# One kernel of attention and routed experts: new instruction ranks, an earlier strike, contiguous list columns and a halved eviction

## The chip, the cores and the metric

The kernel runs on one core of one Trainium2 chip. Its time is the device time of one launch in microseconds (us). Three runs of the kernel before gave 716.53, 718.13 and 720.70 us; the median is 718.13. The engines are called as in the profile: PE (TensorE's matmuls), PEld (its weight loads), DVE (VectorE), ACT (ScalarE), POOL (GpSimd) and SP (SyncE, which only issues DMAs).

## The reference

Inputs: q, k, v of 8 batches x 8 heads x 576 positions x 64, a gate of 512 x 8, and two weight tensors of 8 experts (512 x 1024 and 1024 x 512), all fp32.

```python
# attention: a coarse one on means of 4 positions, and a local one
q_d, k_d, v_d = (t.reshape(B, H, Sd, 4, D).mean(axis=3) for t in (q, k, v))
out_up = np.repeat(sm_attn(q_d, k_d, v_d), 4, axis=2)
mask = np.abs(pos[:, None] - pos[None, :]) < 4          # 7 neighbours
out_local = softmax(where(mask, scale * q @ k.T, -1e9)) @ v
x = (out_up + out_local) -> (4608 tokens, 512)
# experts: all (token, expert) logits in falling order; a token goes to the
# first expert that has room (576 places each)
for idx in np.argsort(-(x @ w_gate).flatten()):
    tok, e = idx // E, idx % E
    if assigned[tok] >= 0 or counts[e] >= cap: continue
    assigned[tok] = e; counts[e] += 1
out[mask_e] = np.maximum(x[mask_e] @ w1[e], 0) @ w2[e]
```

So every token gets one expert, every expert exactly 576 tokens, and who gets which depends on all logits at once.

## The kernel before

**Two stages.** Class `Attention` works through 8 batches and 36 units of 128 tokens. Per batch it loads q, k, v, transposes q and k, forms sums of four and does the coarse attention, whose result goes to a DRAM tensor `up_dram`. Per unit it loads the windows of v (stream W), computes local scores (S), transposes (T), products with v and the normalisation (V), loads the repeated coarse rows (P, `load_up`), adds them (A, on DVE, for units 27 to 33 on POOL), stores x (D) and computes logits (X). Stream Z0 prepares the routing of units 0 to 25 while the attention still runs, Z1 that of the last ten.

The second stage takes the experts in the order in which they fill up. For k = 0 to 7: `Routing.pre` (stream S: row maxima m of the logits, sortable integers s, their high and low halves spread by ACT into xh and xl, one-hot masks, first compares), `phase` (R: a search for the threshold at which the first expert is full, in three levels of 64, 32 and 32 on the high half and three on the low half; each level compares, counts on PE, clips the counts (cs, line 832), sums them on PE, finds the first full one (un) and feeds the next threshold), then `emit` or, for k = 0, `emit_first`: ranks of the chosen tokens, two one-hot tables (ohh from the rank's high part, ohl from its low part), and 18 or 36 matmuls of them (the list) that put the token numbers in order. `gather` (G) fetches the tokens' rows on POOL, five chunks of 128, 128, 128, 128 and 64; `rows` (X) scales them to fp16 high and low parts; `weights` (L) loads and `split` (W) splits the expert's weights the same way (ACT the high, DVE the low part, 8 tiles); `first` (H), `relu` (E), `second` (C) and `store` (Y) are the expert itself: three products (high-high, high-low, low-high) for each layer, ReLU with a new split on ACT and DVE, eviction by ACT, and a scatter by POOL.

**The strike.** When expert k is full, its column is taken out of the logits: DVE makes the mask es (line 1048), POOL multiplies it by -1e30 (line 1060) and adds it to all logits (line 1061). This stands in `end`, which comes after the ranks; `left` (line 1044) is called before them. The next expert's row maxima (line 912) read the logits.

**The order of the work.** Each stream is a generator whose steps are cut by `yield`. `KEYS` holds one rank for each step of each stream; `Plan.run` always takes the step of lowest rank and, through `need`, first whatever this step depends on. In the first stage this order holds for all engines, in the second for PE, DVE, ACT and SP, while POOL's order is left to the framework's planner. Each engine executes its own instructions in the order in which they were issued. A step beyond the end of its stream's ranks gets the last rank plus 0.01 for each further step (`key`). Z0 has 16 steps, Z1 11.

**The first list.** In `emit_first` the low one-hot table is laid out with the low position outside and the token column t inside, so the weights of matmul t are `ohl[:, :, t]`, every 36th element; the compare is made in two halves of 18 columns (`EH`). The tile is lent from the expert's `ht`. FILL gives numbers of matmuls without use that keep TensorE busy while the routing waits.

**The eviction.** `Experts.store` scales each chunk out of PSUM on ACT (line 1419). The last chunk of an expert has 64 rows, computed in two halves of PSUM's partitions, so DVE adds the second half (line 1422). Then POOL scatters the rows.

Of the kernel before, what the change touches and what calls it, by code (L numbers as in the profile page):

```python
# [710 lines left out]
class Routing:  # L711
# [68 lines left out]
    def lend(self, raw):  # L780
# [3 lines left out]
        self.ohw, self.lent = raw[:, :128].bitcast(BF), (raw[:, 82:100].bitcast(BF), raw[:, 100:136].bitcast(BF))  # L784
# [190 lines left out]
    def phase(self, plan, k):  # L975
# [68 lines left out]
        def left():  # L1044
            nc.vector.tensor_tensor(rem, cl, low[0], op=OP.subtract)

        def end(rank):
            nc.vector.tensor_scalar(es, self.code, code, None, op0=OP.is_equal)
# [10 lines left out]
            if k < E - 2:  # L1059
                nc.gpsimd.tensor_scalar(self.pen, es, -1e30, None, op0=OP.mult)  # L1060
                nc.gpsimd.tensor_tensor(self.lg, self.lg, self.pen[:, None].to_broadcast([128, NT, E]), op=OP.add)
# [74 lines left out]
    def emit_first(self, plan, ph, pl):  # L1136
# [9 lines left out]
        ohl = self.ohw  # L1146
        p = self.ps.tile([128, 72], F32, name="pR", bufs=2)[:, :36]
        for i, (a, b) in enumerate(EH):
            if i:
                yield  # L1150
            nc.vector.tensor_tensor(ohl[:, :32, a:b], pl[:, None, a:b].to_broadcast([128, 32, b - a]), self.slot[:, :, a:b],
                                    op=OP.is_equal)
            yield
            self.fill("half" if i else "list")
            for t in range(a, b):
                nc.tensor.matmul(p, ohl[:, :, t], r[:, :, :, t], start=t == 0, stop=t == NT - 1)
# [43 lines left out]
class Experts:  # L1200
# [210 lines left out]
    def store(self, k):  # L1411
# [3 lines left out]
        for c, (s0, n) in enumerate(SL):  # L1415
# [3 lines left out]
            nc.scalar.activation(y[:n], p[:n], AF.Copy, scale=sc)  # L1419
            if n < 128:  # L1420
                yield
                nc.vector.scalar_tensor_tensor(y[:n], p[64:], sc, y[:n], op0=OP.mult, op1=OP.add)
# [756 lines left out]
```

## Time and profile before

| | |
|---|---|
| median of three runs | 718.13 us |
| profiled execution | 716.23 us |
| its span, first to last instruction | 714.6 us |
| PE busy | 674.7 us (94%) |
| PEld busy | 487.5 us |
| DVE busy | 485.8 us (68%) |
| ACT busy | 349.0 us |
| POOL busy | 248.4 us |
| HBM read, written | 93.08 MB, 21.23 MB |
| attention, routing of the first expert, experts (starts) | 0, 257.5, 281.3 us |

The busy time of an engine is the sum of its instructions' durations; matmuls overlap, so a PE that is busy is not one at its peak. In a row of the timeline the brackets at the end give the idle time of the engine before the instruction and what ended it. "PEclk" is the clock that TensorE was granted, as a share of 2.4 GHz. A line number (L1347) is that of the kernel before.

### The profile page before, as it was taken

How to read it: one execution, taken by the hardware profiler on the slowest of the kernel's cores; microseconds unless marked ns; L12 is line 12 of the kernel's file. 1: busy time of each engine (PE TensorE's matmuls, PEld its weight loads, DVE VectorE, ACT ScalarE, POOL GpSimd, SP SyncE). 2: the span in 40 equal slices, each digit the busy share in tenths (PEclk: the TensorE clock that was granted, in tenths of full speed). 3: DMA queues.
4: the chain of work that ended last, by engine and by line, in shares of the span. 5: the costliest groups of instructions: out<-in, count | busy, mean ns of one | idle time of the engine just before them, and what ended most of it. 6: DMA issues, size and time to landing. Idle time of an engine off the chain costs nothing.

```text
span 714.6 us, 19791 instructions
## 1 busy us (share of the span) xinstructions
PE 674.7 (94%) x8031; PEld 487.5 (68%) x8031; DVE 485.8 (68%) x1284; ACT 349.0 (49%) x692; POOL 248.4 (35%) x295
## 2 busy tenths in 40 slices
PE   6999999999999988799999989999999999999994
PEld 4888888898888866574575566576575674764741
DVE  5677777666767666899998798797796776510300
ACT  6587688687686532434435153353442463411310
POOL 7477284537564521204223140330511504102011
PEclk9699999999999976999999999999999999999998
DMA  7799899898898733517774452760931994301001
GB/s 209 203 246 248 231 285 256 262 264 216 258 236 244 224 122 134 169 39 264 135 264 117 176 189 61 274 150 14 337 98 50 407 215 128 72 1 53 15 30 37
DMA packets 142723, 123.86 MB, mean 173 GB/s; under 512 B 86752, under 2 KB 116960, under 8 KB 142632
## 3 DMA queue, kind: packets, MB, share of 16 engines
q1 hardware_dynamic: 135256, 100.82, 49.7%
q0 software_dynamic: 6512, 21.24, 9.4%
q8 instruction: 63, 1.03, 0.6%
q10 hardware_dynamic: 864, 0.54, 0.3%
q14 instruction: 28, 0.23, 0.1%
HBM read 93.08 MB, written 21.23 MB: 160 GB/s over the span
## 4 chain that ended last, share of the span: by engine, by line
PE 51%; issue 18%; DVE 11%; DMA 9%; ACT 4%; POOL 3%; SPq 1%; POOLq 0%; ACTq 0%; DVEq 0%
PE pX L1402 15%; PE pH L1347 14%; DMA up<-up_dram 6%; PE g L502 3%; PE o L554 2%; PE g L353 2%; DMA nat<-in_k_dram 2%; POOL out_dram L1423 2%; PE g L593 2%; PE g L531 2%; PE g L292 2%; PE pR L828 2%; ACT kt L271 1%; PE g L607 1%; DVE x L576 1%
## 5 line engine op out<-in xcount | busy, mean ns | idle before, releaser
L1347 PE MATMUL pH<-xt,wh 128*128 128x256 f16 (+1 forms) x1024 | 192.6, 288 | 2.8 <-DVE ht L1379 2.8
L1402 PE MATMUL pX<-wh,ht 128*128 128x512 f16 (+1 forms) x640 | 183.0, 379 | 0.0
L1347 PE MATMUL pH<-xt,wl 128*128 128x320 f16 (+1 forms) x512 | 145.2, 288 | 0.0
L1402 PEld LDWEIGHTS <-ht 128*128 128x128 f16 (+1 forms) x960 | 81.6, 100 | 87.3 <-issue 3.0
L1402 PE MATMUL pX<-wl,ht 128*128 128x512 f16 (+1 forms) x320 | 117.9, 380 | 0.0
L1423 POOL DMA_INDIRECT out_dram<-y,idx x40 | 43.3, 1081 | 210.6 <-ACT y L1419 193.7
L1347 PEld LDWEIGHTS <-wh 128*128 128x128 f16 x1024 | 95.3, 98 | 29.9 <-DVE ht L1379 3.8
L1375 ACT ACTIVATE ht<-pH 128x512 f16<-128x512 f32 (+1 forms) x128 | 45.5, 407 | 119.5 <-PE pH L1347 106.3
L1379 DVE SCALAR_TENSOR_TENSOR ht<-pH,ht 128x512 f16<-128x512 f32 (+1 forms) x128 | 52.3, 450 | 60.8 <-ACT ht L1375 60.6
L1256 DVE SCALAR_TENSOR_TENSOR wl<-nat,wh 128x512 f16<-128x512 f32 x128 | 86.4, 684 | 4.5 <-ACT wh L1251 3.9
L1279 POOL DMA_INDIRECT xg<-x_dram,idx x40 | 47.4, 1186 | 81.6 <-issue 34.5
L1251 ACT ACTIVATE wh<-nat 128x1024 f16<-128x1024 f32 x64 | 67.0, 1056 | 6.8 <-DMA nat<-in_moe_w_dram 6.0
L1419 ACT ACTIVATE y<-pX 128x512 f32<-128x512 f32 (+1 forms) x40 | 23.8, 596 | 92.2 <-PE pX L1402 55.9
L1347 PEld LDWEIGHTS <-wl 128*128 128x128 f16 x512 | 50.4, 98 | 13.2
L258 POOL TENSOR_TENSOR gtmp<-qz 64x576 f32<-64x576 f32 x28 | 32.8, 1172 | 64.3 <-ACT qz L340 39.3
L539 ACT COPY pt<-g 64x512 f32<-64x512 f32 x72 | 41.6, 580 | 15.3 <-PE g L531 13.6
L502 PE MATMUL g<-kt,qz 128*64 128x38 f32 x1152 | 44.0, 232 | 1.2 <-ACT kt L271 0.8
L502 PEld LDWEIGHTS g<-kt,qz 128*64 128x64 f32 x1152 | 43.0, 145 | 3.2 <-issue 1.7
L554 PE MATMUL o<-vw,pt 128*64 128x65 f32 x1152 | 43.4, 224 | 0.2 <-DMA nat<-in_k_dram 0.2
L292 PE MATMUL g<-ident,nat 128*128 128x128 f32 x256 | 36.7, 281 | 4.9 <-DMA nat<-in_k_dram 3.9
L554 PEld LDWEIGHTS o<-vw,pt 128*64 128x64 f32 x1152 | 37.9, 137 | 5.1 <-issue 4.2
L271 ACT COPY kt<-g 64x512 f32<-64x512 f32 x50 | 31.4, 630 | 7.4 <-PE g L292 6.5
(225 smaller groups left out, 1121.3 us busy)
## 6 DMA issues: line engine op xcount, KB each, us to landing
nat<-in_moe_w_dram SPq DMA_DIRECT2D x28, 1024.0 KB
vw<-in_v_dram SPq DMA_DIRECT2D x136, 78.0 KB
up<-up_dram SPq DMA_DIRECT2D x36, 256.0 KB
x_dram<-x SPq DMA_DIRECT2D x36, 256.0 KB
nat<-in_q_dram SPq DMA_DIRECT2D x16, 512.0 KB
nat<-in_k_dram SPq DMA_DIRECT2D x16, 512.0 KB
nat<-in_v_dram SPq DMA_DIRECT2D x16, 512.0 KB
up_dram<-xu SPq DMA_DIRECT2D x16, 128.0 KB
```

Of the source, the lines that this page charges most:

```text
L292: nc.tensor.transpose(p[:, a, :, fp], src[:, 4 * hh + 2 * a + s, 2 * fp:2 * fp + 2].rearrange("p f d -> p (f d)"), self.ident)
L502: nc.tensor.matmul(sv[64 * a:64 * a + 64, 4 * g + c], self.qz[b % 2][:, 2 * g + a, w].rearrange("p s q -> p (s q)"), self.kt[b][:, 2 * g + ...
L539: nc.scalar.copy(out[r, :, :, a], p[r].rearrange("p (i h q) -> p i h q", h=4, q=QW))
L554: nc.tensor.matmul(o[64 * i:64 * i + 64, g, 65 * h:65 * h + 65], pt[:, 2 * g + i, h].rearrange("p b q -> p (b q)"), self.vw[u % 4][:, i, 4 ...
L1251: nc.scalar.activation(hi, r, AF.Copy, scale=sc)
L1256: nc.vector.scalar_tensor_tensor(lo[:, a:a + LOP], r[:, a:a + LOP], sc, hi[:, a:a + LOP], op0=OP.mult, op1=OP.subtract)
L1279: self.fetched = self.nc.gpsimd.indirect_dma_start(out=xg[:n], out_offset=None, in_=self.x, in_offset=bass.IndirectOffsetOnAxis(ap=idx[:n, ...
L1347: nc.tensor.matmul(p[:, s, :s1 - s0], self.w[k, d][a][:, 128 * f:128 * f + 128], self.xt[k][:, b, d, s0:s1], start=j == 0, stop=j == len(s ...
L1375: nc.scalar.activation(hi, q, AF.Relu)
L1379: nc.vector.scalar_tensor_tensor(lo, q, 0.0, hi, op0=OP.max, op1=OP.subtract)
L1402: nc.tensor.matmul(p[o:o + m], self.ht[k][:, f, h0:h0 + m], self.w[k, 4 + f // 2][b][:, 512 * (f % 2):512 * (f % 2) + 512], start=j < part ...
L1423: i = nc.gpsimd.indirect_dma_start(out=self.out, in_=y[:n], in_offset=None, out_offset=bass.IndirectOffsetOnAxis(ap=plan.vals["idx", k][:n ...
```

## The change

Four edits of code and a new table. (1) The instruction that makes es and the two POOL instructions of the strike go from `end` to the beginning of `left`. (2) In `emit_first` the low one-hot table is laid out with the token column outside, so that the 128 weights of matmul t are contiguous; 32 of them are its own, the other 96 belong to the next columns, and what they produce in PSUM isn't read. The first half's matmuls stop three columns early, since a matmul reads three columns further. (3) The last chunk of the last expert is evicted in two halves of 256 columns. (4) All ranks in `KEYS` are replaced, those of the attention by a table in which Z0 has 11 entries and Z1 nine.

```diff
-        self.ohw, self.lent = raw[:, :128].bitcast(BF), (...)
+        self.ohw, self.lent = raw[:, :36].rearrange("p i t -> p (i t)").bitcast(BF), (...)
...
         def left():
+            nc.vector.tensor_scalar(es, self.code, code, None, op0=OP.is_equal)
+            if k < E - 2:
+                nc.gpsimd.tensor_scalar(self.pen, es, -1e30, None, op0=OP.mult)
+                nc.gpsimd.tensor_tensor(self.lg, self.lg, self.pen[:, None].to_broadcast([128, NT, E]), op=OP.add)
             nc.vector.tensor_tensor(rem, cl, low[0], op=OP.subtract)
         def end(rank):
-            nc.vector.tensor_scalar(es, self.code, code, None, op0=OP.is_equal)
...
-            if k < E - 2:
-                nc.gpsimd.tensor_scalar(self.pen, es, -1e30, None, op0=OP.mult)
-                nc.gpsimd.tensor_tensor(self.lg, self.lg, self.pen[:, None].to_broadcast([128, NT, E]), op=OP.add)
...
-        ohl = self.ohw
+        ohl = self.ohw[:, :32 * NT].rearrange("p (t i) -> p t i", i=32)
...
-            nc.vector.tensor_tensor(ohl[:, :32, a:b], pl[:, None, a:b].to_broadcast([128, 32, b - a]), self.slot[:, :, a:b],
-                                    op=OP.is_equal)
+            nc.vector.tensor_tensor(ohl[:, a:b], pl[:, a:b, None].to_broadcast([128, b - a, 32]),
+                                    self.io[:, None, :].to_broadcast([128, b - a, 32]), op=OP.is_equal)
...
-            for t in range(a, b):
-                nc.tensor.matmul(p, ohl[:, :, t], r[:, :, :, t], start=t == 0, stop=t == NT - 1)
+            for t in range(max(0, a - 3), b if i else b - 3):
+                nc.tensor.matmul(p, self.ohw[:, 32 * t:32 * t + 128], r[:, :, :, t], start=t == 0, stop=t == NT - 1)
...
-            nc.scalar.activation(y[:n], p[:n], AF.Copy, scale=sc)
+            cols = [slice(0, 512)] if n == 128 or k < E - 1 else [slice(0, 256), slice(256, 512)]
+            for w in cols:
+                nc.scalar.activation(y[:n, w], p[:n, w], AF.Copy, scale=sc)
             if n < 128:
                 yield
-                nc.vector.scalar_tensor_tensor(y[:n], p[64:], sc, y[:n], op0=OP.mult, op1=OP.add)
+                for w in cols:
+                    nc.vector.scalar_tensor_tensor(y[:n, w], p[64:, w], sc, y[:n, w], op0=OP.mult, op1=OP.add)
```

Of the table (598 streams), the entries at the start, cut where "..." stands:

```diff
-    "Z0": [1797, 1807, 1828, 1838, 1843, 1853, 1863, 1869, 1879, 1889, 1900, 1906, 1916, 1922, 1925, 1942],
+    "Z0": [1822, 1835, 1842, 1849, 1860, 1866, 1878, 1882, 1895, 1905, 1908],
-    "S0": [2, 9],
+    "S0": [2, 3],
-    "R0": [0, 1, 3, 4, 5, 6, 7, 8, 10, 11, 12, ...
+    "R0": [0, 1, 4, 5, 6, 7, 8, 9, 10, 11, 12, ...
-    "S1": [59, 61, 64, 66, 69, 73, 75, 78, 79, 81, 84, 91],
+    "S1": [57, 60, 61, 63, 66, 67, 69, 70, 73, 75, 80, 86],
-    "R1": [94, 95, 101, 103, 104, 107, 108, 110, 112, ...
+    "R1": [84, 85, 92, 95, 96, 99, 104, 108, 110, ...
-    "X0": [70, 72, 76, 77, 80, 82, 83, 85, 89, 90, 93, 97, 100, 102, 105, 106],
+    "X0": [74, 76, 78, 79, 81, 82, 83, 87, 90, 91, 93, 97, 98, 101, 106, 107],
-    "H0": [86, 87, 92, 96, 109, 111, 114, 118, 127, ...
+    "H0": [88, 100, 105, 109, 112, 115, 117, 120, 126, ...
```

S1.0 is the row maxima, S1.1 the integers, S1.4 the masks, S1.8 the masked maxima, S1.10 and S1.11 the first compares; R1.2 is the first clip of counts (cs), R1.6 the next threshold and its compare; X0.2, X0.5, X0.8, X0.11 and X0.14 are the low parts of the five gathered chunks, H0.0 the first matmuls of expert 0.

For the later experts, what the two tables put between the rank matmul of expert k (step R.38) and its list (R.43), read off by sorting the ranks: PE's steps of six matmuls, and DVE's steps of other streams ahead of the list's compare (R.42). "C" are second-layer steps, "c" those of the last, narrow chunk.

| k | PE before | DVE before | PE after | DVE after |
|---|---|---|---|---|
| 1 | 5 H, 2 C | 1 ReLU | 7 H, 2 C | 2 ReLU, row maxima |
| 2 | 7 H, 1 C | 1 ReLU | 10 H | 2 ReLU, row maxima |
| 3 | 1 H, 2 C, 4 c | 2 splits | 4 H, 4 c | 2 splits |
| 4 | 4 C, 4 c | none | 1 H, 2 C, 4 c | none |
| 5 | 5 C | none | 4 H, 10 C, 4 c | 1 ReLU, 1 split |
| 6 | 5 C | none | 2 C, 4 c | none |

## Rows read from the trace of the kernel before

**Rows 1.** Busy time of stretches: length, busy PE, PEld, DVE, ACT, POOL, clock, DMA
```profile
140.00:220.00 80.00, 77.00 (x1522) 68.90 (x1518) 53.58 (x122) 63.73 (x130) 42.24 (x55) 1.00 0.95 251
...
279.00:280.00 1.00, 1.00 (x18) 1.00 (x16) 0.00 (x0) 1.00 (x1) 0.00 (x0) 1.00 1.18 328
...
281.30:298.50 17.20, 12.95 (x102) 9.85 (x100) 14.90 (x39) 6.86 (x12) 8.23 (x9) 0.80 0.67 222
...
298.50:304.20 5.70, 4.56 (x54) 3.04 (x54) 3.65 (x11) 2.38 (x6) 0.00 (x0) 1.00 0.02 3
...
304.20:426.00 121.80, 116.91 (x1056) 75.62 (x1054) 108.02 (x320) 50.43 (x98) 34.94 (x31) 0.99 0.56 173
...
528.00:704.30 176.30, 176.30 (x1240) 108.43 (x1238) 76.95 (x196) 55.67 (x108) 30.32 (x29) 1.00 0.35 104
```

**Rows 2.** Chain that ended last, pieces in order of time: start, length, what
```profile
337.31 1.31 PE pX L1402 x6
...
428.90 2.31 PE pH L1347 x18
```

**Rows 3.** Timeline of the first expert's first counts: start, length, engine, line, operation
```profile
260.35 0.17 DVE L832 TENSOR_SCALAR cs<-pR 128x16 f16<-128x16 f32 x1 [0.32 <-PE pR L828]
...
260.36 0.32 ACT L907 COPY xl<-u 128x160 int16<-128x160 int16 x1
...
262.25 0.49 DVE L791 TENSOR_TENSOR cmp<-xl,first 128x640 bf16<-128x640 int16 x1
```

**Rows 4.** Timeline around the strike, first expert (three rows) and fifth expert (two)
```profile
276.19 0.23 DVE L1093 SCALAR_TENSOR_TENSOR at<-rank,f 128x72 f32<-128x72 f32 x1
...
285.32 0.81 POOL L1061 TENSOR_TENSOR lg<-lg,pen 128x288 f32<-128x288 f32 x1
...
286.16 0.45 DVE L912 TENSOR_REDUCE m<-lg 128x36 f32<-128x288 f32 x1 [1.15 <-POOL lg L1061]
...
457.43 0.80 POOL L1061 TENSOR_TENSOR lg<-lg,pen 128x288 f32<-128x288 f32 x1
...
457.46 0.81 DVE L1054 TENSOR_TENSOR n<-n,ad 128x36 f32<-128x36 f32 x1
```

**Rows 5.** All instructions of line 1054: duration ns least/median/most, first and last start
```profile
L1054 DVE TENSOR_TENSOR n<-n,ad x7: 195/816/820, 283.0 to 555.9; 128x36 f32<-128x36 f32 x7
```

**Rows 6.** Weight loads of the list (line 1156) and of one count (line 828)
```profile
L1156 PEld LDWEIGHTS <-ht x36: 139/145/173, 278.6 to 281.0; 128*128 128x128 bf16 x36
...
L828 PEld LDWEIGHTS <-cmp x18: 95/96/98, 307.0 to 307.6; 128*128 128x128 bf16 x18
```

**Rows 7.** Timeline of the first expert's list: column compare and list matmuls
```profile
278.07 0.82 DVE L1151 TENSOR_TENSOR ht<-pl,ht 128x576 bf16<-128x576 int16 x2
...
278.63 2.67 PE L1156 MATMUL pR<-ht 128*128 128x36 bf16 x36 [0.41 <-ACT ht L1143]
```

**Rows 8.** Timeline of the fifth expert's list: rank matmul, column compare
```profile
453.48 0.20 PE L1079 MATMUL pR<-f,one 128*128 128x72 bf16 x1
...
458.80 1.35 DVE L1116 TENSOR_TENSOR ohl<-pl,io 128x1152 bf16<-128x1152 int16 x1
```

**Rows 9.** TensorE's waits from 298.5 to 704 us: total, times, longest
```profile
PE pH L1347 <- DVE ht L1379: 2.8, 4, 0.9
...
PE pR L1120 <- DVE ohl L1116: 2.4, 2, 1.6
```

**Rows 10.** Timeline of the last chunk's eviction
```profile
704.42 0.59 ACT L1419 ACTIVATE y<-pX 64x512 f32<-64x512 f32 x1 [2.12 <-PE pX L1402]
...
705.04 0.69 DVE L1422 SCALAR_TENSOR_TENSOR y<-pX,y 64x512 f32<-64x512 f32 x1 [22.54 <-ACT y L1419]
```

**Rows 11.** Timeline of the attention's last units: up-row load, normalisation, last addition
```profile
249.29 0.52 SPq L471 DMA_DIRECT2D up<-up_dram  x1
...
249.85 0.21 DVE L565 RECIPROCAL rx<-o 128x8 f32<-128x8 f32 x1 [1.75 <-PE o L554]
...
254.49 0.69 DVE L576 TENSOR_TENSOR x<-x,up 128x512 f32<-128x512 f32 x1 [0.66 <-DMA up<-up_dram]
```

More of the change, by code (lines that the diff above doesn't have):

```diff
@@ L783, in lend @@
         self.slot, self.t128f = raw[:, 32:64].bitcast(I16), raw[:, 64:82].bitcast(BF)
-        self.ohw, self.lent = raw[:, :128].bitcast(BF), (raw[:, 82:100].bitcast(BF), raw[:, 100:136].bitcast(BF))
+        self.ohw, self.lent = raw[:, :36].rearrange("p i t -> p (i t)").bitcast(BF), (raw[:, 82:100].bitcast(BF), raw[:, 100:136].bitcast(BF))
         nc.scalar.copy(self.slot, self.io[:, :, None].to_broadcast([128, 32, NT]))
```

1164 rows, old and new, of the table KEYS are left out of this document.

## The prediction

> **What bounds the kernel now.** I read the stretches first [rows 1]. In the middle of the attention TensorE is busy 77.00 of 80 us and the DMA engines 0.95, so neither leaves room. From 528 to 704.3 us TensorE is busy all the time at full clock: the last experts are a fixed amount of matmul work, and only an earlier start of it, or a shorter tail, can move the end. Between lie three stretches with holes: 281.3 to 298.5 us, where VectorE works 14.90 of 17.20 us and TensorE waits for its products; 298.5 to 304.2, where TensorE lacks 1.14 us; and 304.2 to 426, where it lacks 4.89 us. Next the chain of waits [rows 2]: from 300 us on it is nearly all matmuls, and its pieces give the units I count with: six second-layer matmuls take 1.31 us (half of that in an expert's last, narrow chunk, which runs two side by side), six first-layer ones 0.77 (18 in 2.31). Last I read single rows where the diff touches the order.
>
> **The change part by part.** All sums start from the profiled execution: span 714.6 us, 1.63 us around it, 716.23 us in all. The median of the runs is 718.13, 1.90 above it; I add the sum to the median.
>
> *The moved step S0.1.* Expert 0's leftover compare of the low halves (10 columns, VectorE) goes in the experts' table from rank 9 to rank 3, so on VectorE ahead of the first clipping of counts (cs, R0.2). It reads the low halves that ScalarE spreads at 260.36; they are there at 260.68. VectorE runs cs at 260.35 now [rows 3]. Behind the compare (0.49 us) cs starts at about 261.24: +0.9 us, and everything of expert 0's routing is queued behind it (the clip feeds TensorE, which feeds the next threshold, and so on to the list). Where the compare stands now, beside a TensorE count, it costs nothing, so nothing comes back. At the least, if ScalarE spread them earlier, the compare still fits only partly into the 0.32 us that VectorE idles there: +0.2. I take +0.9.
>
> *Strike ahead of the list.* The expert's column is struck from the logits by two POOL instructions that now follow the threshold search. Removed: the 0.81 us pass between two gathers, and VectorE's 1.15 us of idleness before expert 1's row maxima, which waited for that pass [rows 4]. Added: for expert 0 the pass runs at about 275.8 to 276.6, beside the ranks. What POOL does there to VectorE is seen at the fifth expert [rows 4]: while the pass runs (457.43, 0.80 us), an addition of 36 columns takes 0.81 us instead of 0.20 (the seven of them range from 0.195 to 0.820 [rows 5]). In its new place the next instruction of that kind, with two operands in SBUF, is the one at 276.19; I take +0.4, between nothing and the 0.62 measured. For experts 1 to 5 both places lie ahead of the list's compare on VectorE, so the loss only changes its place: 0. The comparison that makes the expert's mask (es, 0.23 us) is moved into VectorE's idle wait for a TensorE product: 0.
>
> *Contiguous columns.* 36 weight loads now read every 36th element: 145 ns each, started 69 ns apart (278.6 to 281.0); those of the count, contiguous, take 96 ns, 35 ns apart [rows 6], both at a granted clock of 1.0, that is 2.4 GHz, or close to it [rows 1]. 36 x 34 ns = 1.2 us less on TensorE. Against it VectorE builds the columns with the position repeated along the inner axis; the row that has this form does 1152 elements in 1.35 us, so half of it takes 0.67, against 0.41 now (two in 0.82) [rows 7, 8]. The first half is then ready at 278.75, not 278.5 (TensorE starts at 278.63, on a ScalarE product), the second at 279.4, when TensorE has just done its 15 columns; the list would end near 280.3 instead of 281.3. I take -1.0. Bounds: +0.3 if the loads don't become faster, -1.2 if VectorE is hidden.
> The Trainium skill (TensorE: Matmul & The Clock Gate, section on the weight-path perf modes) says that the fast weight load takes 128 weights of a 16-bit type packed or strided alike. By that rule the strided loads should not have been slower, the edit would give nothing on TensorE, and the sum would be 1.3 us higher; the 145 against 96 ns above speak against it, though both rows differ in more than the stride (36 against 16 moving columns).
>
> *Start of the experts.* Up to here the list of expert 0 is at +0.9 +0.4 -1.0 = +0.3 us. The gathers then follow each other 1.25 us apart, without the strike's two instructions; but chunks 2 to 4 wait for VectorE, not for their rows. VectorE gets 1.15 us of idleness back, less the 0.3. The new table spends it on expert 1's maxima, masks and compares, which now stand ahead of the low parts of the gathered chunks (S1.8 to S1.11 and R1.2 to R1.6): by my count in table order the chunks' low parts come at the same times as now, the first matmul block is some 1.5 us later, and expert 1's search 2 us earlier. That removes most of the 1.14 us that TensorE lacks between 298.5 and 304.2, where it waits for this search. Net at 304 us: -0.5; bounds -1.5 (all the idleness and the holes) and +1.0 (the late block, holes kept).
>
> *The experts' table after that.* TensorE's waits there are for VectorE: list compares (2.4 us, the longest 1.6, fourth expert) and products of ReLU (2.8 us in four) [rows 9]. From the rank matmul to the end of the list's compare VectorE needs 6.67 us (453.48 to 460.15, fifth expert [rows 8]). To that come the ReLU products (0.81 us), row maxima (0.45) and weight splits (0.68) that a table puts between; against it stand the matmuls that TensorE has between its rank matmul and the list (counted in the table of covers under "The change"). For the table of before this gives holes of 1.0, 0.8, 2.0, 0, 0.1 and 0 us for the second to the seventh expert, and the profile has the second's and the fourth's together as 2.4, the third's as a ReLU wait of 0.9, and none for the others: the count works. For the new one: second, 8.0 us of matmuls against 6.67 + 1.62 + 0.45 = 8.7, a hole of 0.7 (-0.2 against the count of before); third 7.7 against 8.7 (+0.2); fourth 5.7 against 8.0 (+0.3); fifth 6.0 against 6.7 (+0.6, now uncovered); sixth none; seventh 5.2 against 6.05, since no strike stretches an addition there (+0.7). That is +1.6. Of the ReLU waits 0.8 us may go with the weight splits that are ranked later. Sum +0.8; bounds -4.9 (all of TensorE's holes) and +2.5 (no ReLU wait goes, another comes).
>
> *Halved eviction.* The last chunk of the last expert leaves by ScalarE 0.59 us, then VectorE 0.69 [rows 10]; in halves VectorE's first half runs beside ScalarE's second. At most half of 0.59 goes; a second start on each engine takes part of it: -0.15 (bounds -0.3 and +0.1).
>
> *The attention's table.* The ranks of the two tables differ by 8 to 17 places (standard deviation) within stretches of 100, with no drift: a reshuffle over about two units. With TensorE and DMA as full as [rows 1] shows, I take 0. Either way the price is one landing of an up-row load more or less on the chain: the one that ends the attention is issued at 249.29 and lets the last addition start at 254.49 [rows 11], so -5.2 to +5.2.
>
> Sum: -0.5 + 0.8 - 0.15 + 0 = +0.15 us: 716.4 against the profiled time, 718.3 against the median. About 0.5% (3.6 us) is what a measurement can tell from no change here: 714.5 to 721.7 is "same".
>
> **The rivals.**
> 1. *The experts' table clears the holes.* Later weight splits leave VectorE to lists and ReLU; all 4.89 us of [rows 1] can't go, 4 would, in place of the +0.8: 713.5. For it: the waits are for VectorE, which is busy 108 of 122 us there, and the splits of weights are ranked later. Against: the covers counted above. 0.20.
> 2. *The attention loses one landing*: 718.3 - 5.2 = 713.1. For it: the last unit waits on such a load. Against: the DMA engines can't move the same bytes sooner. 0.07.
> 3. *Slower: VectorE stands at an early compare.* The older table has 11 entries for Z0, the code 16 steps; the last five follow each other without anything between. So VectorE has "u", then at once two compares that need POOL's spreads, and POOL is in additions that wait for up-row loads. Behind the compares stands the normalisation of unit 34, at 249.85 now, ahead of which VectorE idles 1.75 us [rows 11]. A delay of it by about 1 us is hidden, since the last addition waits until 254.49 for its load; it decides once the loads ahead of POOL's additions land over a microsecond later, and then, as each up-row buffer is released by an addition, costs up to a landing: 718.3 + 5.2 = 723.5. 0.15. The experts' stage at its upper bounds (+2.5 after 304 us and +1.0 before, in place of +0.3) comes near it: 721.5, and with half a microsecond from elsewhere over the line, 0.10.
> 4. *The stride was not the cost*: the contiguous columns do not do what they are for; 718.3 + 1.3 = 719.6. For it, what the rows differ in beside the stride. 0.08.
>
> **How the numbers follow.** My own forecast, no change within 715 to 721, has 0.40. With rival 4: same 0.48. Faster: 0.20 + 0.07 = 0.27. Slower: 0.15 + 0.10 = 0.25. The range takes in the rivals to their points and about a microsecond beyond on either side, for the terms' own bounds: 711.8 to 724.4.
>
> **What would show it.** In the changed trace: the clip of expert 0's first counts behind the leftover compare, some 0.9 us later after the routing's start; an addition or rank instruction of expert 0 stretched beside POOL's pass; the list's loads near 35 ns apart and its two compares at 0.67 us; no idleness before expert 1's row maxima; a wait of TensorE for the list compare of the fifth expert (0.6 us) and the seventh (0.8); the last chunk's two engines overlapping. I'm wrong if the attention ends more than 3 us away from 257.5, or if TensorE's holes after 304 us sum to less than 3 or more than 8 us.

## The result and the profile after

| | median of 12 runs | range | profiled execution, span | busy PE / DVE / POOL |
|---|---|---|---|---|
| before | 719.49 us | 716.53 to 721.52 | 716.23, 714.6 us | 674.7 / 485.8 / 248.4 us |
| after | 724.15 us | 720.25 to 732.67 | 720.33, 718.7 us | 674.3 / 488.9 / 243.4 us |

The ratio of after to before is 1.0071, 95% interval [1.0045, 1.0096]: +5.1 us [3.2, 6.9] on 720 us, slower. The forecast was no change. A run more than 1.5% above the fastest of its kernel (here the 732.67) is left out of every ratio, and no time is read from the profile of such a run (the late new ranks below).

The attention's end (the start of the last copy of logits, line 610) wanders: 257.3 to 263.9 us in profiles of kernels with the attention code and ranks of before, and 269.3 us in one that was run only once. So two profiles can't be compared by their ends. I split each at that copy and call the profiled time behind it the rest: before 716.23 - 257.31 = 458.9 us, after 720.33 - 258.12 = 462.2. The three other kernels with the second stage's code and ranks of before came to 458.1, 459.6 and 459.7, so theirs agree within 1.6 us. The second stage of after agrees less well with itself: 462.2 here, 461.9 and 459.6 in two more kernels that have it (below). So of after's loss 0.7 to 3.3 us lie behind the attention by the profiles.

The stretches of [rows 1] in the changed kernel (length, busy PE, PEld, DVE, ACT, POOL, granted clock, DMA share, GB/s):

```profile
281.30:298.50 17.20, 12.12 (x117) 9.58 (x115) 15.09 (x40) 7.06 (x13) 7.14 (x7) 0.90 0.71 246
298.50:304.20 5.70, 5.56 (x66) 4.15 (x65) 3.39 (x11) 1.77 (x5) 0.00 (x0) 1.00 0.04 15
304.20:426.00 121.80, 116.54 (x1034) 74.73 (x1032) 101.43 (x310) 49.32 (x98) 31.65 (x31) 0.99 0.56 172
528.00:704.30 176.30, 175.18 (x1230) 108.00 (x1229) 77.94 (x197) 56.06 (x110) 27.67 (x28) 1.00 0.36 107
```

The 1.14 us that TensorE lacked between 298.5 and 304.2 are 0.14 now, as forecast. But it lacks 5.26 us from 304 to 426 (4.89 before) and 1.12 where it lacked nothing; from 304.2 to 704.3 us it lacks 7.7 us in all, 5.8 before. What it waits for from 300 to 707 us (total, times, longest) is VectorE still:

```profile
PE pH L1347 <- DVE ht L1379: 2.6, 6, 1.0
PE pR L836 <- DVE cs L832: 2.0, 4, 1.0
PE pR L1120 <- DVE ohl L1116: 2.0, 1, 2.0
```

Against [rows 9] the list waits are one long wait instead of two, and the ReLU waits hardly shrank. The waits for the clipped counts (cs) doubled, from 1.0 us in three:

```profile
PE pR L836 <- DVE cs L832: 1.0, 3, 0.4
```

The rows around the first list, for [rows 3, 4, 6, 7]:

```profile
261.22 0.49 DVE L791 TENSOR_TENSOR cmp<-xl,first 128x640 bf16<-128x640 int16 x1 [0.39 <-ACT xl L907]
261.67 0.17 DVE L832 TENSOR_SCALAR cs<-pR 128x16 f16<-128x16 f32 x1
...
277.06 0.79 POOL L1048 TENSOR_TENSOR lg<-lg,pen 128x288 f32<-128x288 f32 x1
277.50 0.43 DVE L1093 SCALAR_TENSOR_TENSOR at<-rank,f 128x72 f32<-128x72 f32 x1
...
279.59 1.42 DVE L1151 TENSOR_TENSOR ht<-pl,io 128x576 bf16<-128x576 int16 x2
280.40 2.56 PE L1156 MATMUL pR<-ht 128*128 128x36 bf16 x36 [1.16 <-DVE ht L1151]
283.00 0.17 DVE L1160 COPY odd<-pR 32x18 f32<-32x18 f32 x1 [1.99 <-PE pR L1156]
...
285.82 0.45 DVE L912 TENSOR_REDUCE m<-lg 128x36 f32<-128x288 f32 x1
L1156 PEld LDWEIGHTS <-ht x36: 96/118/125, 280.4 to 282.6; 128*128 128x128 bf16 x36
```

The clip (cs) stands behind the compare; `at` takes 0.43 us beside POOL's pass, not 0.23; the list waits for the dearer compare (1.42 for two halves, 0.82 before) and is itself hardly shorter (2.56 us, 2.67 before), though each weight load takes 118 ns, not 145; the row maxima (m) no longer wait. From `at` to the copy behind the list it is 5.50 us, 5.15 before.

The eviction, for [rows 10]: from ScalarE's start to VectorE's end 1.45 us, 1.31 before. The engines don't overlap: VectorE's first half starts at 709.06, behind both of ScalarE's (708.38 + 0.64).

```profile
708.38 0.64 ACT L1421 ACTIVATE y<-pX 64x256 f32<-64x256 f32 x2 [2.12 <-PE pX L1402]
709.06 0.77 DVE L1425 SCALAR_TENSOR_TENSOR y<-pX,y 64x256 f32<-64x256 f32 x2 [22.60 <-ACT y L1421]
```

### The profile page after: what moved, and what is told of

It reads as the page before. It is cut to its first block, busy times and chain, and to the rows that moved or that the text cites. A ratio compares the mean times of both kernels' runs of the same rounds, so it can differ in the third digit from the quotient of the medians.

```text
span 718.7 us, 19798 instructions
## 1 busy us (share of the span) xinstructions
PE 674.3 (94%) x8031; PEld 483.7 (67%) x8031; DVE 488.9 (68%) x1285; ACT 349.1 (49%) x693; POOL 243.4 (34%) x295
## 4 chain that ended last, share of the span: by engine, by line
PE 54%; issue 16%; DVE 13%; ACT 8%; DMA 4%; POOL 2%; SPq 1%; another core or an unknown queue 1%; POOLq 0%; DVEq 0%; ACTq 0%
PE pX L1402 15%; PE pH L1347 15%; PE o L554 3%; PE g L502 3%; ACT kt L271 3%; PE g L292 2%; POOL out_dram L1426 2%; PE g L353 2%; PE g L531 2%; PE g L607 2%; PE g L593 2%; DMA up<-up_dram 2%; PE pR L828 1%; ACT qz L271 1%; DVE wl L1256 1%
## 5 line engine op out<-in xcount | busy, mean ns | idle before, releaser
L1347 PE MATMUL pH<-xt,wl 128*128 128x256 f16 (+1 forms) x512 | 145.0, 287 | 0.0
L1426 POOL DMA_INDIRECT out_dram<-y,idx x40 | 41.4, 1034 | 216.9 <-ACT y L1421 192.9
L1279 POOL DMA_INDIRECT xg<-x_dram,idx x40 | 44.4, 1111 | 65.2 <-DVE idx L1133 26.4
L1421 ACT ACTIVATE y<-pX 128x512 f32<-128x512 f32 (+2 forms) x41 | 23.8, 584 | 85.2 <-PE pX L1402 54.1
L539 ACT COPY pt<-g 64x512 f32<-64x512 f32 x72 | 41.8, 580 | 15.5 <-PE g L531 12.5
L554 PE MATMUL o<-vw,pt 128*64 128x65 f32 x1152 | 43.6, 224 | 3.3 <-issue 2.2
L502 PE MATMUL g<-kt,qz 128*64 128x38 f32 x1152 | 42.4, 228 | 2.1 <-ACT kt L271 1.5
L502 PEld LDWEIGHTS g<-kt,qz 128*64 128x64 f32 x1152 | 41.1, 140 | 4.0 <-ACT kt L271 1.6
L554 PEld LDWEIGHTS o<-vw,pt 128*64 128x64 f32 x1152 | 38.2, 137 | 7.8 <-issue 6.2
L271 ACT COPY qz<-g 64x512 f32<-64x512 f32 x52 | 32.1, 617 | 3.7 <-PE g L292 2.8
```

The costliest lines, as they stand in the source:

```text
L271: self.nc.scalar.copy(out, in_)
L502: nc.tensor.matmul(sv[64 * a:64 * a + 64, 4 * g + c], self.qz[b % 2][:, 2 * g + a, w].rearrange("p s q -> p (s q)"), self.kt[b][:, 2 * g + ...
L554: nc.tensor.matmul(o[64 * i:64 * i + 64, g, 65 * h:65 * h + 65], pt[:, 2 * g + i, h].rearrange("p b q -> p (b q)"), self.vw[u % 4][:, i, 4 ...
L1279: self.fetched = self.nc.gpsimd.indirect_dma_start(out=xg[:n], out_offset=None, in_=self.x, in_offset=bass.IndirectOffsetOnAxis(ap=idx[:n, ...
L1347: nc.tensor.matmul(p[:, s, :s1 - s0], self.w[k, d][a][:, 128 * f:128 * f + 128], self.xt[k][:, b, d, s0:s1], start=j == 0, stop=j == len(s ...
L1426: i = nc.gpsimd.indirect_dma_start(out=self.out, in_=y[:n], in_offset=None, out_offset=bass.IndirectOffsetOnAxis(ap=plan.vals["idx", k][:n ...
```

## Experiments: the change taken apart

Four kernels hold one part each or leave one out. T1: the older attention ranks carry the loss. T2: the experts' ranks do. T3: the code edits do. Each ratio and difference is against the kernel before run in the same set, where its median was 719.7 to 720.7 us.

```diff
-KEYS = BEFORE
+KEYS = {s: (AFTER if attention(s) else BEFORE)[s] for s in BEFORE}
```

Older attention ranks alone. 

> The kernel before, with the older attention ranks alone (no code edit, the experts' ranks of before). T1, the attention carries the loss: the profiled run of the changed kernel ends its attention only 0.8 us later, but its median run is 4 us above the profiled one, and those runs differ in the attention, at the low clock; so this kernel takes most of the 5 us: +3 to +5.5 us against the kernel before, with runs that spread by 8 us or more. T2, the experts' table carries it: +0.8 us or less. T3, the code edits carry it: 0 to +0.8. The rival of the prediction (a forfeited up-row landing behind the clump of early compares) would give +5.2 in every run, and show as the end of the attention near 262.5 us.

```diff
-KEYS = BEFORE
+KEYS = {s: (BEFORE if attention(s) else AFTER)[s] for s in BEFORE}
```

Experts' ranks alone. 

> The kernel before, with the new experts' ranks alone (the leftover compare S0.1 ahead of the clip; no code edit, the attention ranks of before). T1: 0 to +1 us. T2: +2.5 to +3 us, of which 0.5 is S0.1 ahead of the first clip and 2 the list compares that TensorE waits for after 304 us; holes of TensorE after 304 us sum to about 6 to 7 us, against 5.7 before. T3: 0 to +1.

```diff
-KEYS = AFTER
+KEYS = BEFORE
```

Code edits alone (this diff and the next are against the changed kernel). 

> The kernel before, with the code edits alone (strike ahead of the list, contiguous columns, halved eviction; both tables of ranks as before, so that S0.1 stands behind the clip). T1: 0 +- 1 us. T2: +0.3 (+0.2 from the addition that the strike stretches, +0.1 to +0.2 from the list, eviction 0), less what the search of the second expert wins from VectorE's 1.15 us: -0.8 to +0.4. T3: +2 or more: the ranks of before don't fit the new place of the strike.

```diff
-KEYS = AFTER
+KEYS = {s: (BEFORE if attention(s) else AFTER)[s] for s in BEFORE}
```

Code edits and experts' ranks. 

> The changed kernel with the attention ranks of before (that is, code edits and experts' ranks together). T1: 0 to +1.5 us and a spread like that of the kernel before (5 us). T2: +2.5 to +3.3 us. T3: as the code edits alone, +2 or more. If parts add up, its difference is that of the two kernels above it together.

| kernel | median | ratio to before | difference | rest behind the attention |
|---|---|---|---|---|
| attention ranks alone | 724.24 | 1.0046 [1.0024, 1.0068] | +3.3 us | 459.6 us |
| experts' ranks alone | 728.42 | 1.0117 [1.0074, 1.0160] | +8.4 us | 467.3 us |
| code edits alone | 717.13 | 0.9963 [0.9937, 0.9988] | -2.7 us | 455.4 us |
| code edits, experts' ranks | 724.86 | 1.0053 [1.0021, 1.0084] | +3.8 us | 461.9 us |
| all (after) | 724.15 | 1.0071 [1.0045, 1.0096] | +5.1 us | 462.2 us |

T3 falls: the code edits gain. T2 was right in its place and too small in size: laid on the code edits the experts' ranks cost 3.8 + 2.7 = 6.5 us in the times (some 3 us either way) and 461.9 - 455.4 = 6.5 us in the traces. Without the early strike they cost 8.4, which the intervals don't tell from 6.5. The row maxima wait longer for the strike there, 1.75 us against 1.15, but they start 4.82 us behind the list's copy (281.34 before, 286.47 here) as before. What comes later is the first gathered chunk's low part (xt), behind the second expert's masked maxima now: 11.3 us behind the copy,

```profile
291.29 0.45 DVE L912 TENSOR_REDUCE m<-lg 128x36 f32<-128x288 f32 x1 [1.75 <-POOL lg L1061]
...
297.74 0.68 DVE L1307 SCALAR_TENSOR_TENSOR xt<-pX,xt 128x512 f16<-128x512 f32 x1
```

against 10.0 in the kernel before:

```profile
291.35 0.68 DVE L1307 SCALAR_TENSOR_TENSOR xt<-pX,xt 128x512 f16<-128x512 f32 x1
```

T1 was right in part: the attention ranks alone cost 3.3 us, nearly all of it ahead of the last copy, since the rest (459.6) is that of before (458.9) within the scatter. One way to add up the loss is -2.7 (code) + 6.5 (experts' ranks) + 1.3 (attention ranks, the last row less the fourth; its interval is some 3 us either way). The section on the clump has a kernel that doesn't fit this sum.

## Experiments: the code edits and the first list

```diff
         def left():
+            (es, and the strike's two POOL instructions, moved here from end)
             nc.vector.tensor_tensor(rem, cl, low[0], op=OP.subtract)
```

The strike's place alone. 

> The kernel before with the strike ahead of the list alone (strided columns, whole eviction, both tables of ranks as before). U1, the strike's place is what the code edits gain by: from the end of the first list to the last matmul 418.5 us or less, against 423.0 before and 418.5 with all three edits, and -2.5 to -4 us in the time. U2, the contiguous columns or the eviction are: 422 to 423 us there, and 0 to +0.3 us in the time. In both cases the first list from the addition named at to its end takes 5.35 us (5.15 before, 5.49 with all three edits).

Measured: 717.15 us, ratio 0.9967 [0.9928, 1.0005], rest 453.7 us, 417.5 us from the copy behind the list to the last matmul, 5.37 us from `at` (279.48) to the copy (284.85). U1: the strike's place is what the edits gain by; the columns and the eviction add nothing (717.13 with them). The second expert's row maxima start 3.4 us behind the copy and no longer wait, 4.8 before:

```profile
288.27 0.45 DVE L912 TENSOR_REDUCE m<-lg 128x36 f32<-128x288 f32 x1
```

Its price is `at` beside POOL's pass (+0.20 us, 0.4 forecast); the columns add 0.13 us more (5.50).

Why don't the columns help? Two kernels measure the pitch (the distance of two starts), with matmuls without use ahead of the list's own (100 weights) or between them (128). Each was run once; only the pitch is read from it.

```diff
+            w0, m0 = self.one[:, :100], self.one[:, :36]
+            for w in (w0, strided), m in (m0, r[:, :, :, t]):
+                36 x nc.tensor.matmul(hot, w, m, start=True, stop=True)
```

> The code edits alone (ranks of before), with four times 36 matmuls without use ahead of the first list's first half: 100 weights contiguous or every 36th element, 36 moving columns contiguous or every 36th element, in the order both contiguous, weights strided, columns strided, both strided; TensorE is at full clock there. The list's own matmuls start 69 ns apart with strided weights and 65 ns apart with contiguous ones, and in both kernels their moving columns are strided. The prediction's step (the stride of the weights is the cost): 36 matmuls take 1.3 us with contiguous weights, 2.4 us with strided ones, whatever the columns are. P, the moving columns' stride is: 1.3 us, 1.3 to 1.5, 2.3, 2.4. Q, neither is, it is the size (36 columns and the wait for PSUM): about 2.3 us all four.

With 100 weights (start to start, 36 each): both contiguous 46 ns at full clock, weights strided 177 (the clock falls within it), columns strided 87 at half clock, both strided 178. None of the three forecasts came. With 100 weights their stride is dear; the list's 66 to 69 ns are not of this kind. The second kernel took the same with 128 weights, 18 matmuls of a kind, in the order given:

> As the pitch run before it, but with full sets of 128 weights, 18 matmuls of each kind, between the two halves of the first list, in the order both contiguous, both strided, columns strided, weights strided, both contiguous again. With 100 weights the stride cost 130 ns each (46 ns a matmul contiguous, 177 strided, whatever the clock). If the load of 128 is another, stride-blind one, as the list's 69 and 65 ns have it: strided weights with contiguous columns take at most 10 ns more than contiguous ones (35 to 46 ns at full clock), and the strided columns carry the rest, 60 to 70 ns with either weights. If the weights' stride costs with 128 too: 60 ns or more with contiguous columns.

The timeline (start, length) and the stretches' clock (the figure after POOL's):

```profile
292.04 0.63 PE L1159 MATMUL pX<-one 128*128 128x36 bf16 x18
292.51 1.43 PE L1161 MATMUL pX<-ht 128*128 128x36 bf16 x18
293.77 1.39 PE L1163 MATMUL pX<-ht,one 128*128 128x36 bf16 x18
294.97 1.22 PE L1165 MATMUL pX<-one,ht 128*128 128x36 bf16 x18
296.03 0.70 PE L1167 MATMUL pX<-one 128*128 128x36 bf16 x18
296.57 1.56 PE L1169 MATMUL pR<-ht 128*128 128x36 bf16 x21
...
292.51:293.70 1.19, 1.19 (x24) 1.19 (x20) 0.00 (x0) 1.06 (x1) 0.00 (x0) 0.99 0.89 361
293.77:294.90 1.13, 1.13 (x21) 1.13 (x19) 0.00 (x0) 0.00 (x0) 0.00 (x0) 0.50 0.75 297
294.97:296.00 1.03, 1.03 (x21) 1.03 (x19) 0.00 (x0) 1.01 (x1) 0.00 (x0) 0.50 0.14 56
296.03:296.50 0.47, 0.47 (x19) 0.47 (x18) 0.00 (x0) 0.02 (x1) 0.00 (x0) 0.50 0.00 0
```

Divide the distance of two kinds' starts by 18: both contiguous 26 ns (30 at half clock), both strided 70 (full clock), columns alone 67 and weights alone 59 (half clock). Either stride costs about 30 to 45 ns and they don't add; making one operand contiguous leaves the other to set the pace. The list's columns (`r[:, :, :, t]`) are strided in both kernels, so 69 ns became 66 there, at full clock and at half clock alike; weights alone were not measured at full clock. By the Trainium skill (TensorE: Matmul & The Clock Gate, weight-path perf modes) the fast load of 128 weights takes them packed or strided. What the stride costs isn't said there, so reading it as free, as the prediction did, went beyond it; here it is 59 against 30 ns at the same clock.

## Experiments: the experts' ranks and the clock

The ranks were spliced at the second expert's gather, on the code edits and the attention ranks of before.

```diff
-KEYS[experts] = AFTER
+KEYS[experts] = AFTER up to G1 (rank 225), then the order of BEFORE
```

> All three code edits, the attention ranks of before, and of the experts' ranks the new ones up to the gather of the second expert (G1), from there on the order of before. V1, the new table loses in the start of the experts (the second expert's maxima and compares ahead of the gathered chunks): the second list stands 43.8 us after the first one's end, as with the whole new table, against 42.9 with the old one, and nothing more is lost behind it: 419.4 us to the last matmul, +0.9 us against the code edits alone, -2 us against before. V2, it loses as much again by a low clock at 9 to 15 us behind the first list: +1.5 to +2.2 us against the code edits alone.

```diff
-KEYS[experts] = AFTER
+KEYS[experts] = BEFORE up to G1 (rank 222), then the order of AFTER
```

> All three code edits, the attention ranks of before, and of the experts' ranks the old ones up to the gather of the second expert, from there on the new order. The whole new table takes 424.8 us from the first list's end to the last matmul, the old one 418.5. V1: the late part carries little, 419 to 421 us, -1 to -3 us against before. V2: it carries +4.5 to +5.5 us, with a hole of 2.0 us at the fourth expert's list and a low clock for 3.5 us behind it: 423 to 424 us, +1.5 to +2.5 us against before.

New ranks early: 717.76 us, 0.9978 [0.9948, 1.0008], -1.6 us, rest 457.5. New ranks late: 719.13 us, 0.9984 [0.9945, 1.0023], -1.2 us. Against the code edits alone (-2.7) the parts cost +1.1 and +1.5 us by the times, each uncertain by some 3, while both together cost 6.5. The times don't place the loss, and between V1 and V2 they don't decide: the late part's time is V1's, and the early part's trace has V2's low clock (6.8 us of it, from 10.9 us behind the copy). The traces show what the loss is made of. From the code edits to the code edits with the experts' ranks the stretch from the copy to the last matmul grows from 418.5 to 424.8 us; in it TensorE stands 1.9 us longer and works 6.8 us more at half clock (10.2 against 3.4), of which at most half is lost, 3.4 us by this estimate. TensorE's hole ahead of the fourth expert's list, in the changed kernel, and the stretches behind it:

```profile
413.46 0.76 PE L1120 MATMUL pR<-r,ohl 128*128 128x72 bf16 x18 [1.96 <-DVE ohl L1116]
...
409.00:414.00 5.00, 3.04 (x41) 1.64 (x38) 4.83 (x15) 2.45 (x6) 0.00 (x0) 1.00 1.02 401
414.00:418.00 4.00, 3.67 (x25) 2.45 (x22) 3.76 (x14) 1.21 (x2) 1.60 (x2) 0.66 1.07 389
```

Behind the hole TensorE works at half clock for some 3 us. What that costs is seen from the first matmul of the fourth list to that of the fifth, with the same order of work: 51.2 to 51.3 us where the clock fell, 49.85 in a kernel where it stayed up; with the ranks of before 49.2 to 49.3 against 48.0. So such a hole costs 1.2 to 1.5 us again. It doesn't always: with holes of 1.96 us or more the clock fell here in three profiles of four, with 1.26 to 1.57 us in three of nine (one is the kernel before). So three kernels fill holes with matmuls without use.

```diff
+        for _ in range(50 if k == 3 else 0):
+            nc.tensor.matmul(p, self.one, self.one[:, :72], start=True, stop=True, skip_group_check=True)
         for t in range(0, NT, 2):
             nc.tensor.matmul(p, ohl[:, t:t + 4]...
```

On the late new ranks: 

> The kernel of late new ranks (code edits, old ranks to the second expert's gather, new ones behind it) with 50 matmuls without use (72 columns each) ahead of the fourth expert's list, where TensorE stood 1.96 us for VectorE and then ran 3.4 us at half clock. W1, the hole costs twice, once in its length and again by the clock that falls behind it: TensorE stands 0.6 us or less there, the clock stays at 1.00 at 131 to 135 us behind the first list, and the stretch from the first list's end to the last matmul falls by 1.5 to 1.9 us from 423.5. W2, the low clock there has another reason (it follows the power or the time, not the hole): it stays low, and the stretch stays at 423 to 424 us. The list itself isn't earlier in either case.

```profile
412.75 1.80 PE L1120 MATMUL pR<-one 128*128 128x72 bf16 x50
...
414.78 0.76 PE L1122 MATMUL pR<-r,ohl 128*128 128x72 bf16 x18 [0.23 <-DVE ohl L1116]
...
415.49:419.49 4.00, 3.47 (x29) 2.56 (x28) 3.76 (x15) 1.50 (x3) 1.77 (x2) 1.00 1.08 388
```

The clock stayed up, and the list isn't earlier, as W1 has it. From the fourth list's first matmul to the fifth's it takes 49.85 us, so it saves the 1.4 to 1.5 us against a fallen clock. But it is one profile, and one of the four without filler kept its clock too, so that the filler kept it isn't shown. The time is 719.12 us, 0.9961 [0.9931, 0.9990], against 719.13 without: in the time nothing can be told.

On the strike alone, 34 of them, ranks of before: 

> The strike alone (ranks of before) with 34 matmuls without use ahead of the fourth expert's list, where TensorE stands 1.26 us. In its profile the clock stayed up behind that hole, in that of another kernel with the same hole it fell for 3 us. W1: the profiled stretch stays at 417.5 +- 0.5 us, and the median falls by 0 to 1 us against the strike alone: -2.5 to -4 us against before. W2: no change against the strike alone, or +0.3 us where the fillers run into the list.

```diff
-XFILL = (22, 5, 8)
+XFILL = (22, 5, 20)
```

And with this as well: 

> As the one above, and 12 more matmuls without use (256 columns each, 0.11 us) ahead of the first expert's third chunk, where TensorE stands 1.66 us for VectorE; in six of the ten profiles the clock is low for 3 to 7 us behind that place. W1: no low clock between 8 and 18 us behind the first list, the profiled stretch 417.5 us +- 0.5, and the median 0.5 to 1.5 us below the strike alone: -3 to -5 us against before, the fastest of all. W2: no change against the strike alone.

714.61 us, 0.9885 [0.9837, 0.9933], and 714.60 us, 0.9897 [0.9854, 0.9941]: 8.3 and 7.4 us faster than before by the ratio, 5.5 by the medians, more than was expected. Both beat the kernel before and the changed one. Their rests, 455.1 and 453.7 us, are no shorter than the strike's 453.7, so the profiles don't show what they gained over it; the intervals meet. The profiled stretch of the second is 417.5 us, and between 8 and 18 us behind the first list the clock is 1.00; that of the first is 418.9 (W1 had 417.5), with 0.83 there. The strike alone, without fillers, had 417.5 and 1.00 there as well.

```profile
294.58:304.58 10.00, 8.50 (x97) 6.62 (x95) 8.41 (x19) 2.89 (x7) 2.23 (x3) 1.00 0.69 243
```

```profile
295.24:305.24 10.00, 7.39 (x64) 5.58 (x64) 8.45 (x17) 2.84 (x6) 2.21 (x3) 0.83 0.71 244
```

The filler at the first expert's chunk adds nothing to the median (714.60 against 714.61, six runs each), where W1 had a gain; with intervals of some 3 us this decides nothing.

## Experiments: the clump of early compares

```diff
-KEYS = BEFORE
+KEYS = {s: (AFTER if attention(s) and s not in ("Z0", "Z1") else BEFORE)[s] for s in BEFORE}
```

> The kernel before with the older attention ranks, but the two streams that prepare the routing (Z0 and Z1) ranked as before. With their older ranks the time was +3.3 us [+1.7, +4.9]. The prediction's rival, VectorE standing at the clump of early compares: 0 to +1.3 us here. If it is the rest of the older table (or nothing in particular): +2 to +4.5 us, the same as with all older ranks.

```diff
-KEYS = AFTER
+KEYS = {s: (BEFORE if s in ("Z0", "Z1") else AFTER)[s] for s in AFTER}
```

On the changed kernel: 

> The changed kernel with the streams Z0 and Z1 ranked as before. From the end of the attention to the end of the launch it takes 462 us as the changed kernel does (458.9 before). Z1, the clump of early compares costs 2 to 3 us in the attention, as the pair of kernels with older attention ranks (+3.3, and +0.4 without the clump) has it: +2.5 to +3.5 us against before. Z2, it costs less than 1 us, and that pair differed by chance: +4 to +5.5 us.

```diff
-KEYS = BEFORE
+KEYS = {s: (AFTER if s in ("Z0", "Z1") else BEFORE)[s] for s in BEFORE}
```

These two streams alone: 

> The kernel before with the older ranks of the streams Z0 (11 entries) and Z1 (9) alone; every other rank and all code as before. Two pairs of kernels differ by these ranks in the other surroundings: +3.3 against +0.4 us, and +5.1 against 0.0. Z1, the clump of early compares costs by itself: +2 to +5 us, with the last eight units' logits taking 14.5 to 15.5 us (12.6 to 14.3 in the profiles of the old ranks), and the stretch behind the attention as before (458 to 460 us). Z3, it costs only together with the other older attention ranks: 0 +- 1.5 us, and 12.6 to 14.3 us there.

| ranks beside the clump | without the clump | with it |
|---|---|---|
| older attention ranks, before's code | 719.87, 1.0005 [0.9975, 1.0034] | 724.24, 1.0046 |
| all of after | 720.18, 0.9999 [0.9967, 1.0031] | 724.15, 1.0071 |
| all of before | 1 | 724.44, 1.0057 [1.0023, 1.0092] |

Three pairs, +3.0, +5.2 and +4.1 us: the older ranks of Z0 and Z1 cost by themselves, and with before's code the other attention ranks nothing that can be told (+0.4 us [-1.8, +2.5]).

The second row doesn't fit the sum above. Code edits, experts' ranks and the other attention ranks together come to -0.1 us [-2.4, +2.2], where code edits and experts' ranks alone came to +3.8 [1.5, 6.0]. So either the other attention ranks gain some 4 us on the changed code, which no kernel tests, or the 6.5 us of the experts' ranks are too much. The rest of this kernel is 459.6 us (462 was expected): its hole ahead of the fourth list is the same 1.96 us, but the clock didn't fall behind it. How the loss divides between the clump and the experts' ranks stays open by some 4 us. The trace of the older Z0 and Z1 ranks alone shows how the clump costs (start, length, [idle before]):

```profile
251.50 1.91 DVE L791 TENSOR_TENSOR nat<-xh,first 128x1152 bf16<-128x1152 int16 x2
251.87 1.22 PE L554 MATMUL o<-vw,pt 128*64 128x65 f32 x32
253.56 0.66 POOL L905 COPY xl<-u 128x288 int16<-128x288 int16 x2 [1.10 <-DVE u L950]
254.01 2.21 DVE L791 TENSOR_TENSOR nat<-xl,first 128x1152 bf16<-128x1152 int16 x2 [0.52 <-POOL xl L905]
256.15 0.19 DVE L565 RECIPROCAL rx<-o 128x8 f32<-128x8 f32 x1
256.38 0.69 DVE L567 TENSOR_TENSOR x<-o,rx 128x512 f32<-128x512 f32 x1
257.17 2.09 PE L554 MATMUL o<-vw,pt 128*64 128x65 f32 x32 [2.93 <-issue]
...
257.15:260.20 3.05, 3.03 (x36) 2.64 (x36) 0.87 (x2) 0.00 (x0) 0.00 (x0) 0.50 0.19 72
```

VectorE goes through two compares of both halves, waiting for POOL's spread between, before it normalises a unit (rx, then the product L567). The last unit's products (L554) start 0.10 us behind that (256.38 + 0.69 to 257.17), and as closely in both other kernels with the clump: the normalisation frees what they write to, by the times; the row names no releaser. They start 5.30 us behind those of the unit before, and TensorE then works at half clock. The same distance is 4.56 us in the changed kernel and 4.87 with the older attention ranks, but 2.24 in the kernel before and 2.31 in both kernels without the clump:

```profile
254.37 1.24 PE L554 MATMUL o<-vw,pt 128*64 128x65 f32 x32 [1.07 <-ACT xt L599]
255.65 0.21 DVE L565 RECIPROCAL rx<-o 128x8 f32<-128x8 f32 x1 [1.41 <-PE o L554]
256.68 1.25 PE L554 MATMUL o<-vw,pt 128*64 128x65 f32 x32
256.90 1.09 DVE L791 TENSOR_TENSOR nat<-xl,first 128x1152 bf16<-128x1152 int16 x2
```

(older attention ranks, Z0 as before: the normalisation goes ahead of the second compare.) So 2.3 to 3.1 us of the 3 to 5 are seen in these rows; the half clock adds to it where it falls. The last eight units' logits took 16.6 us here (14.5 to 15.5 expected) and 12.4 to 14.6 in the profiles without the clump. The rest is open.

## Why the prediction was wrong

Two terms of the sum failed and a third was missing.

- **"The attention's table ... I take 0."** The ranks have no drift, but the clump, which I had as the third rival at 0.15, was there. Its mechanism came as described, except that the price is not a landing of an up-row load (5.2 us): it is a unit's product that VectorE doesn't fetch and TensorE's next one behind it, 2.3 to 3.1 us. I took a delay of the normalisation of about 1 us as hidden, because the last addition waited for its load. The delay is 3.1 us (the products end at 251.87 + 1.22, the normalisation starts at 256.15), and TensorE's next products wait for it too.
- **"The experts' table after that ... Sum +0.8."** With the moved S0.1 the ranks were to cost 1.7 us; they cost 6.5 on the code edits (some 4 less, if the kernel without the clump is right). Of the list waits counted, the fourth's came (1.96 us), the seventh's by half (0.42), those of the second, third and fifth not. The ReLU waits, of which 0.8 us was to go, stayed (2.6 against 2.8), and the waits for clipped counts, for which there was no term, went from 1.0 to 2.0. And no term had the clock, the one that was missing: holes were priced at their length, and with these ranks TensorE worked 6.8 us more at half clock.
- **"Contiguous columns ... I take -1.0."** +0.13 in the trace. The weights' stride does cost (59 against 30 ns), but behind the like cost of the columns' stride (67), which the sum left out: the list's matmuls went from 69 to 66 ns, not to 35. So rival 4's result came for another cause than the one it named. The bound +0.3 held.
- **The moved S0.1, +0.9.** The clip follows the last copy of logits by 3.5 to 3.8 us in all five kernels with the new rank and by 3.04 in the kernel before: +0.5 to 0.7. (Two with the old rank show 3.5 and 3.6 as well; why is open.)
- **The strike.** Stretch of `at` +0.20 (0.4 forecast). The gain was undersized: the start was -0.5 with the list at +0.3, so -0.8 for the strike and the new order behind the list. The strike alone gives -2.4 us [-5.2, +0.4] in the times, all code edits -2.7 [-4.5, -0.9]. From the copy to the last matmul four profiles with the second stage of before take 422.3 to 423.7 us and four with the early strike and the ranks of before 417.5 to 418.8, that is 3.4 to 6.2 less. Part of it is the clock: TensorE works 10.2 us at half clock there in the kernel before and 2.0 with the strike alone.
- **Halved eviction, -0.15:** +0.14, just outside its bounds, because VectorE's first half waited for both of ScalarE's.

The time, 724.15 us, lies inside the range by 0.25 us, at its end, where the third rival and the experts' upper bounds stood; that it lies inside is luck. Both losses happened, in shares that stay open, and the code edits' gain hid part of them. Neither sign of being wrong showed: the attention ended at 258.1 us in the profile, and the holes after 304 us came to 7.7 us, so the signs were set too wide.

## What to carry to other kernels

Price a wait not by who waits first but by everything that the waiting engine's next instructions release: here VectorE's normalisation held up TensorE's next products. Measure a rank table apart from the code edits that come with it: here the edits gained 2.7 us under the ranks of before, and the new ranks lost 6.5 us on the same edits. Where two strided operands feed small matmuls, as in this list, making one of them contiguous gains little.

## What was not expected of the hardware

- Matmuls of 36 columns with 128 weights: 26 to 30 ns contiguous, 59 with strided weights (half clock), 66 to 67 with strided columns (either clock), 70 with both (full clock); with 100 weights 46 contiguous and 177 strided. At half clock the contiguous ones took 30 ns, hardly more than at full clock.
- VectorE and POOL stretch each other: two compares that took 1.09 us in one profile took 2.21 beside a POOL addition in three, and the addition itself took 1.77 us, not 1.27.
- Behind a hole of 1.96 us or more at one place the granted clock fell in three profiles of four and stayed up in one; with some 50 small matmuls (36 ns each) in the hole it stayed up in the one profile taken. The fall cost 1.4 to 1.5 us.
- The same attention ended between 257.3 and 263.9 us, in one case at 269.3; two single profiles can be compared only stage by stage.
